# Fused causal attention and two-way max MoE on one core: score tiles of a head pair packed into three full PSUM tiles, three score regions per two pairs

## The chip, the cores and the metric

One core of a Trainium2 chip. The metric is the time of one execution on the device, in microseconds (us). Ratios are the mean time of one kernel's fast runs over the mean of the kernel before's fast runs of the same rounds, on the same chip, so they are not quite the ratio of the medians quoted beside them. A run is called slow where it lies over 1.5% above the fastest of its kernel. "Before" and "after" are the kernel without and with the change.

## The reference

Block-causal attention (blocks of 64, 8 batches, 8 heads, 576 positions, head size 64), then a feed-forward layer that takes the maximum of two projections.

```python
scores = scale * np.matmul(q, k.transpose(0, 1, 3, 2))
mask = block_i >= block_j                       # blocks of 64
scores = np.where(mask, scores, -1e9)
attn = np.exp(scores - scores.max(-1)) ; attn /= attn.sum(-1)
x = (attn @ v).transpose(0, 2, 1, 3).reshape(B * S, H * D)      # 4608 x 512
out = np.maximum(x @ w1, x @ w2) @ w_out
```
(Shortened; the kernel works in bf16 with float32 sums.)

## The kernel before

Two heads make a **pair**, 32 pairs in all; two pairs make a **group**. TensorE holds both heads of a pair side by side, one in each half of its 128 rows (64-row form). In the main loop (pairs 4 to 31) every pair goes to the scores twice (each such stretch in the 64-row form is a **visit**), and in between TensorE is filled with feed-forward matmuls of earlier batches (`fill(n)`) and with the attention-value product (`av`) of the pair two steps back. Scores live in two tiles of two banks in PSUM, the memory that TensorE writes its sums to; everything else shares four one-bank PSUM buffers (`ps_m`).

```python
    ps_s = ctx.enter_context(tc.tile_pool(name="ps_s", bufs=2, space=bass.MemoryType.PSUM))
    ps_m = ctx.enter_context(tc.tile_pool(name="ps_m", bufs=4, space=bass.MemoryType.PSUM))
# ... transposes(): two ps_m tiles, 18 small transposes; copy_out() empties the first on
#     VectorE and the second on ScalarE (`copies`)
    def burst_a(p):
        u0 = ps_s.tile([P, 2, 512], FP32, name="ps_s", tag="s")
        scores(p, u0, 0, 0, 0, 512)          # key chunk 0, 512 queries
        u1 = ps_s.tile([P, 2, 512], FP32, name="ps_s", tag="s")
        scores(p, u1, 0, 0, 512, 64)
        scores(p, u1, 64, 1, 128, 448)
        exp(p, u0, 512, 0)
        mask(p, 0)
        exp(p, u1, 512, 512)
        mask(p, 576)

    def burst_b(p):
        u2 = ps_s.tile([P, 2, 512], FP32, name="ps_s", tag="s")
        scores(p, u2, 0, 2, 256, 320)
        scores(p, u2, 320, 3, 384, 192)
        u3 = ps_s.tile([P, 2, 512], FP32, name="ps_s", tag="s")
        scores(p, u3, 0, 4, 512, 64)         # the last 64 keys: a tile of its own
        exp(p, u2, 512, 1024)
        # ... masks
        exp(p, u3, 64, 1536, m=BLK)
# ... main loop, per pair s:
        burst_a(s)
        fill(n_a)
        copy_out = t_pair(s)                 # transposes of the next group's queries or keys
        burst_b(s)
        copy_out()
        pool_work(s)
        if s >= HP + LAG:
            p = s - LAG
            av(p, [0, 1])
            fill(n_b)
            av(p, [2, 3, 4])
        fill(n - n_a - n_b)
```

The softmax here doesn't subtract the row's maximum and nothing guards it: scores larger than these inputs give would overflow.

## Time and profile before

| | before |
|---|---|
| median | 289.32 us (288.81 to 289.93, 3 runs) |
| span of the profiled run | 286.7 us |
| TensorE, VectorE, ScalarE, GpSimd busy | 98%, 65%, 48%, 35% |
| one group of the steady part | 15.56 us |

In profile lines PE is TensorE (PEld its weight loads), DVE is VectorE, ACT is ScalarE, POOL is GpSimd; L420 is a line of the kernel; `[...]` is idle time before an instruction and what the profile thinks ended it.

### The profile page before, as it was taken

Reading aid. Unit: us, or ns where it says so; the run is one execution under the profiler, and the core shown is the slowest. Engines: PE = TensorE matmul, PEld = TensorE weight load, DVE = VectorE, ACT = ScalarE, POOL = GpSimd, SP = SyncE. Lnnn points to the kernel's source line nnn. Section 1 sums busy time; section 2 is a strip of 40 time slices with the busy share of each in tenths; the row PEclk is TensorE's granted clock in tenths of the full one; section 3 lists DMA queues with packets and bytes.
Section 4 is the critical chain, followed back from the end, with each engine's and each line's share of the span. In section 5 each row is a group of like instructions: output and inputs, shape, how many; then the busy total and the mean of one; then the engine's idle time right before and its main releaser. Section 6 shows DMA issues by size and latency. Waiting matters only on the chain.

```text
span 286.7 us, 7670 instructions
## 1 busy us (share of the span) xinstructions
PE 280.0 (98%) x3197; PEld 146.1 (51%) x3197; DVE 186.7 (65%) x390; ACT 137.0 (48%) x194; POOL 101.5 (35%) x243
## 2 busy tenths in 40 slices
PE   7799999999999999999999999999999999999995
PEld 3457666555554545545445445454554554444443
DVE  6867878578785666766665666566665766455430
ACT  3786575775665455555545555545545100010112
POOL 2995547547535432344225532543111000000000
PEclk9999999999999999999999999999999999999999
DMA  7999999977954692479266684555101011011114
GB/s 266 259 210 233 169 259 257 247 231 86 192 133 82 141 144 88 156 77 237 49 201 75 171 115 105 130 59 67 43 37 39 37 39 74 37 63 49 53 60 146
DMA packets 55939, 36.67 MB, mean 128 GB/s; under 512 B 38752, under 2 KB 43232, under 8 KB 55904
## 3 DMA queue, kind: packets, MB, share of 16 engines
q0 software_dynamic: 41728, 7.87, 34.0%
q1 hardware_dynamic: 13760, 27.66, 28.4%
q10 hardware_dynamic: 416, 0.66, 0.7%
q8 instruction: 25, 0.41, 0.6%
q14 instruction: 10, 0.08, 0.1%
HBM read 34.60 MB, written 9.44 MB: 154 GB/s over the span
## 4 chain that ended last, share of the span: by engine, by line
PE 93%; DMA 4%; DVE 1%; POOL 0%; issue 0%; ACT 0%
PE ps_h L196 44%; PE ps_y L214 21%; PE ps_o L398 12%; PE ps_s L319 8%; DMA vv<-in_v_dram 2%; PE ps_qT L302 2%; DMA qraw<-in_q_dram 2%; PE ps_xe L420 2%; PE ps_kT L302 2%; PE ps_w L291 1%; PE ps_y L230 1%; PE ps_xo L422 0%; DVE g L205 0%; DVE xp L405 0%; POOL vv L131 0%; DVE qT L309 0%
## 5 line engine op out<-in xcount | busy, mean ns | idle before, releaser
L196 PE MATMUL ps_h<-xT,w_sb 128*128 128x512 bf16 (+3 forms) x640 | 140.7, 358 | 0.1
L325 ACT ACTIVATE aT<-ps_s 128x1024 bf16<-128x1024 f32 (+3 forms) x128 | 100.3, 832 | 59.5 <-PE ps_s L319 56.9
L196 PEld LDWEIGHTS <-w_sb 128*128 128x128 bf16 x640 | 57.7, 98 | 55.6 <-issue 5.5
L203 DVE CAST h<-ps_h 128x512 bf16<-128x512 f32 (+3 forms) x80 | 50.9, 636 | 44.6 <-PE ps_h L196 42.9
L214 PE MATMUL ps_y<-wo_sb,g 128*128 128x512 bf16 x280 | 69.6, 379 | 0.0
L330 POOL MEMSET aT<- 64x128 bf16 x124 | 22.7, 200 | 107.7 <-ACT aT L325 107.3
L220 ACT COPY y<-ps_y 128x512 f32<-128x512 f32 x31 | 18.2, 586 | 81.3 <-PE ps_y L214 58.8
L205 DVE TENSOR_TENSOR g<-h,ps_h 128x512 bf16<-128x512 bf16 (+3 forms) x80 | 50.5, 631 | 9.1 <-PE ps_h L196 7.4
L398 PEld LDWEIGHTS <-aT 128*128 128x128 bf16 x960 | 33.8, 98 | 14.8 <-DVE xp L405 7.6
L398 PE MATMUL ps_o<-vv,aT 128*128 128x65 bf16 x960 | 40.5, 194 | 0.3
L214 PEld LDWEIGHTS <-g 128*128 128x128 bf16 x280 | 25.5, 98 | 27.6 <-issue 3.2
L319 PE MATMUL ps_s<-qT,kT 64*128 64x64 bf16 (+6 forms) x400 | 34.7, 271 | 0.9 <-ACT kT L309 0.7
L131 POOL DMA_DIRECT2D vv<-in_v_dram x40 | 33.7, 847 | 0.0
L405 DVE TENSOR_TENSOR xp<-ps_o,rec 128x256 bf16<-128x256 f32 (+1 forms) x64 | 31.4, 491 | 2.2
L319 PEld LDWEIGHTS <-kT 64*128 64x128 bf16 x400 | 15.9, 94 | 15.2 <-issue 9.3
L404 DVE RECIPROCAL rec<-ps_o 128x4 f32<-128x4 f32 (+1 forms) x64 | 11.8, 184 | 15.1 <-PE ps_o L398 14.8
L127 POOL CAST qn<-qraw 128x1152 bf16<-128x1152 f32 (+1 forms) x15 | 16.5, 1102 | 7.2 <-DMA qraw<-in_q_dram 4.5
L127 POOL CAST kn<-kraw 128x1152 bf16<-128x1152 f32 x15 | 17.2, 1146 | 3.7 <-DMA kraw<-in_k_dram 2.9
L186 POOL COPY g<-g 128x512 bf16<-128x512 bf16 x8 | 4.9, 614 | 37.9 <-DVE g L205 37.8
L425 DVE COPY xT<-ps_xe 128x640 bf16<-128x640 bf16 (+2 forms) x18 | 8.1, 452 | 11.6 <-PE ps_xe L420 11.1
L309 DVE COPY qT<-ps_qT 128x576 bf16<-128x576 bf16 x17 | 12.9, 757 | 2.0 <-PE ps_qT L302 0.7
L309 DVE COPY kT<-ps_kT 128x576 bf16<-128x576 bf16 x17 | 12.8, 754 | 1.8 <-PE ps_kT L302 0.8
(41 smaller groups left out, 113.9 us busy)
## 6 DMA issues: line engine op xcount, KB each, us to landing
qraw<-in_q_dram SPq DMA_DIRECT2D x16, 576.0 KB, 4.2
out_dram<-y SPq DMA_DIRECT2D x35, 256.0 KB, 2.1
kraw<-in_k_dram SPq DMA_DIRECT2D x15, 576.0 KB, 6.1
vv<-in_v_dram POOLq DMA_DIRECT2D x32, 128.0 KB, 6.7
w_sb<-in_moe_w_dram POOLq DMA_DIRECT2D x4, 256.0 KB, 6.5
w_sb<-in_moe_w_dram POOLq DMA_DIRECT2D x2, 512.0 KB, 10.8
wo_sb<-in_moe_w_out_dram POOLq DMA_DIRECT2D x2, 512.0 KB, 12.0
kraw<-in_k_dram ACTq DMA_DIRECT2D x1, 576.0 KB, 5.4
```

The source lines that it names most:

```text
L127: copy(out=n[:, j0:j1], in_=t[:, j0:j1])
L131: nc.gpsimd.dma_start(out=vv_r[b % NV][:rows, c, :, :D], in_=v[b, :, c * P:c * P + rows, :].rearrange("h p d -> p h d"),)
L196: nc.tensor.matmul(pt[:, :w], w_sb[:, c, f * P:(f + 1) * P], xT[:, c, t0:t0 + w], start=(c == 0), stop=(c == NDM - 1),)
L203: nc.vector.tensor_copy(out=h1[:, :w], in_=pt[:, :w])
L205: nc.vector.tensor_max(g[:, f, m:m + w], h1[:, :w], pt[:, :w])
L214: nc.tensor.matmul(py[:], g[:, f, s * P:(s + 1) * P], wo_sb[:, f, :], start=(f == 0), stop=(f == NFF - 1),)
L309: copies[i](out=t[:, :S].rearrange("q (p j) -> q p j", j=RPP), in_=pts[i].rearrange("q j p -> q p j"),)
L319: nc.tensor.matmul(ps[:m, hh, col:col + w], kT[r, c * P:c * P + m], qT[r, q0:q0 + w], start=True, stop=True,)
L325: nc.scalar.activation(out=aT_r[p % NA][:m, :, a0:a0 + w], in_=ps[:m, :, :w], func=AF.Exp, scale=scale,)
L330: (eng or nc.gpsimd).memset(aT_r[p % NA][BLK:, :, a0:a0 + BLK], 0.0)
L398: nc.tensor.matmul(po[:, gi, hh, :], a[:, hh, a0:a0 + P], vv[:, c, h0 + 2 * hh, :], start=(mm == 0), stop=(mm == n_mm - 1),)
L405: nc.vector.tensor_mul(xp[:, ts[0]:ts[0] + n, :, p % 2], po[:, :, :, :D], rec[:, :n].to_broadcast([P, n, 2, D]),)
```

## The change

The last 64 keys see only the last 64 queries, a 64x64 piece per head that took a whole PSUM tile. Chunk 3 has a corner that the causal mask throws away anyway: its last 64 keys against queries 384 to 447. The change puts the piece there. Two matmuls with zero-padded keys (`kz` = keys 384 to 447, zeros, keys 512 to 575) accumulate the useful upper half and the piece in the lower half. Now a pair fills exactly three tiles, two pairs six, and two tiles make a **region**: three score regions per group instead of four. The attention-value work moves ahead of the transposes and the region.

```diff
+    def pad_keys(p):
+        nc.gpsimd.tensor_copy(  # blocks 0 and 2 of kz <- blocks 6 and 8 of the keys
+    def corner_scores(p, ps, col):
+        qT, kz = qT_r[p % NT], kz_r[p % NT]
+        for k0, q0 in ((0, 384), (BLK, 512)):
+            for hh in range(2):
+                r = slice(hh * D, (hh + 1) * D)
+                nc.tensor.matmul(
+                    ps[:, hh, col:col + BLK], kz[r, k0:k0 + P], qT[r, q0:q0 + BLK],
+                    start=(k0 == 0), stop=(k0 > 0),
+                )
+    def tile_2(p):
+        corner_scores(p, u, 320)
+        scores(p, u, 0, 2, 256, 320)
+        scores(p, u, 384, 3, 448, P)
+        # exp of all 512 columns, and of the corner's lower half to its own place
-    for s in range(HP, NPAIR):
-        burst_a(s) ; fill(n_a) ; t_pair(s) ; burst_b(s) ; av(...) ; fill(...)
+    for g in range(GPB, NG):
+        region(tile_0(a), tile_1(a))
+        lo, hi = n // 18, n * 2 // 9
+        for p, tiles in ((a, lambda: (tile_2(a), tile_0(b))), (b, lambda: (tile_1(b), tile_2(b)))):
+            fill(hi)
+            av_with(p - LAG, lo)             # av [0, 1], fill(lo), av [2, 3, 4]
+            copy_out = t_pair(p)
+            region(*tiles())                 # scores of both tiles, then both exps
+            copy_out()
+            # ... pad_keys for the next group, pool_work
+        fill(n - 2 * (lo + hi))
```
(Cut and joined; also moved: the rows of the last v chunk, some initial memsets, and the casts of queries and keys, now together once per group.)

More of the change, by code (lines that the diff above doesn't have):

```diff
@@ L94 @@
     qT_r = [ring.tile([P, S], BF16, name=f"qT{r}") for r in range(NT)]
-    kT_r = [ring.tile([P, S + APAD], BF16, name=f"kT{r}") for r in range(NT)]
+    kz_r = [ring.tile([P, 3 * BLK], BF16, name=f"kz{r}") for r in range(NT)]
+    kT_r = [ring.tile([P, S], BF16, name=f"kT{r}") for r in range(NT)]
     vv_r = [ring.tile([P, NCH, H, D + 1], BF16, name=f"vv{r}") for r in range(NV)]
@@ L131, in load_v @@
         nc.gpsimd.dma_start(
-            out=vv_r[b % NV][:rows, c, :, :D],
+            out=vv_r[b % NV][P - rows:, c, :, :D],
             in_=v[b, :, c * P:c * P + rows, :].rearrange("h p d -> p h d"),
@@ L161 @@
         nc.vector.memset(vv_r[r][:, :, :, D:D + 1], 1.0)
-        nc.vector.memset(vv_r[r][BLK:, NCH - 1, :, :], 0.0)
+        nc.vector.memset(vv_r[r][:BLK, NCH - 1, :, :], 0.0)
+    for r in range(NA):
+        nc.vector.memset(aT_r[r][:, :, AW:], 0.0)
     for r in range(NT):
-        nc.vector.memset(kT_r[r][:, S:], 0.0)
-    for r in range(NA):
-        nc.vector.memset(aT_r[r][BLK:, :, CB[4] + 512:], 0.0)
-        nc.vector.memset(aT_r[r][:BLK, :, AW:], 0.0)
+        nc.vector.memset(kz_r[r][:, BLK:2 * BLK], 0.0)
     cast("q", 0, ((dve, 0, 7), (pool, 7, RPP)))
@@ L313, in transposes, with scores @@
         return copy_out
-    def scores(p, ps, col, c, q0, w, m=P):
+    def scores(p, ps, col, c, q0, w):
         qT, kT = qT_r[p % NT], kT_r[p % NT]
+        k0 = min(c * P, S - P)
         for hh in range(2):
@@ L319, in scores, with exp @@
             nc.tensor.matmul(
-                ps[:m, hh, col:col + w], kT[r, c * P:c * P + m], qT[r, q0:q0 + w],
+                ps[:, hh, col:col + w], kT[r, k0:k0 + P], qT[r, q0:q0 + w],
                 start=True, stop=True,
             )
-    def exp(p, ps, w, a0, m=P):
+    def pad_keys(p):
+        nc.gpsimd.tensor_copy(
+            out=kz_r[p % NT].rearrange("p (a c) -> p a c", c=BLK)[:, 0:3:2],
+            in_=kT_r[p % NT][:, S - 3 * BLK:].rearrange("p (a c) -> p a c", c=BLK)[:, 0:3:2],
+        )
[7 more added lines that the diff above has]
+                    start=(k0 == 0), stop=(k0 > 0),
+                )
+    def exp(p, ps, w, a0):
         nc.scalar.activation(
-            out=aT_r[p % NA][:m, :, a0:a0 + w], in_=ps[:m, :, :w], func=AF.Exp, scale=scale,
+            out=aT_r[p % NA][:, :, a0:a0 + w], in_=ps[:, :, :w], func=AF.Exp, scale=scale,
         )
@@ L358, in masks_q, with tile_0, tile_1, out @@
             mask(p, a, eng)
-    def burst_a(p):
-        u0 = ps_s.tile([P, 2, 512], FP32, name="ps_s", tag="s")
-        scores(p, u0, 0, 0, 0, 512)
-        u1 = ps_s.tile([P, 2, 512], FP32, name="ps_s", tag="s")
-        scores(p, u1, 0, 0, 512, 64)
-        scores(p, u1, 64, 1, 128, 448)
-        exp(p, u0, 512, 0)
-        mask(p, 0)
-        exp(p, u1, 512, 512)
-        mask(p, 576)
-    def burst_b(p):
-        u2 = ps_s.tile([P, 2, 512], FP32, name="ps_s", tag="s")
-        scores(p, u2, 0, 2, 256, 320)
-        scores(p, u2, 320, 3, 384, 192)
-        u3 = ps_s.tile([P, 2, 512], FP32, name="ps_s", tag="s")
-        scores(p, u3, 0, 4, 512, 64)
-        exp(p, u2, 512, 1024)
-        mask(p, 1024)
-        mask(p, 1344)
-        exp(p, u3, 64, 1536, m=BLK)
+    def tile_0(p):
+        u = ps_s.tile([P, 2, 512], FP32, name="ps_s", tag="s")
+        scores(p, u, 0, 0, 0, 512)
+        return lambda: (exp(p, u, 512, 0), mask(p, 0))
+    def tile_1(p):
+        u = ps_s.tile([P, 2, 512], FP32, name="ps_s", tag="s")
+        scores(p, u, 0, 0, 512, 64)
+        scores(p, u, 64, 1, 128, 448)
+        return lambda: (exp(p, u, 512, 512), mask(p, 576))
+    def tile_2(p):
+        u = ps_s.tile([P, 2, 512], FP32, name="ps_s", tag="s")
+        corner_scores(p, u, 320)
+        scores(p, u, 0, 2, 256, 320)
+        scores(p, u, 384, 3, 448, P)
+        def out():
+            exp(p, u, 512, 1024)
+            nc.scalar.activation(
+                out=aT_r[p % NA][BLK:, :, 1536:AW], in_=u[BLK:, :, 320:320 + BLK],
+                func=AF.Exp, scale=scale,
+            )
+            mask(p, 1024)
+            mask(p, 1344)
+        return out
+    def region(*tiles):
+        for out in tiles:
+            out()
     def av(p, ts):
@@ L433, with fill_of @@
     KEEP = 6
-    def fill_of(s):
-        if s >= NPAIR - LAG:
-            return 27
-        left = 10 - s if s < 10 else 4 - (s - 2) % 4
+    def fill_of(g):
+        if g == NG - 1:
+            return 54
+        left = 5 - g if g < 5 else 2 - (g - 5) % 2
         return -(-max(0, ready() - KEEP) // left)
@@ L448, in pool_work @@
             cast("q", 4, ((pool, 0, RPP),))
+            cast("k", 4, ((pool, 0, RPP),))
         else:
@@ L451, in pool_work @@
                 load_qk(g + 3, (SP, SP), gated=True)
-            if g + 1 + i < NG:
-                cast("kq"[i], g + 1 + i, ((pool, 0, RPP),))
+            if i == 1 and g + 2 < NG:
+                cast("q", g + 2, ((pool, 0, RPP),))
+                cast("k", g + 2, ((pool, 0, RPP),))
             nb, j = divmod(s + 2, HP)
@@ L531 @@
     transposes("k", 2, (dve, act))()
+    pad_keys(4)
+    pad_keys(5)
     fill(2)
@@ L546, with av_with @@
     x_due = []
-    for s in range(HP, NPAIR):
-        g, i = divmod(s, 2)
+    def av_with(p, n):
+        av(p, [0, 1])
+        fill(n)
+        av(p, [2, 3, 4])
+    for g in range(GPB, NG):
+        a, b = 2 * g, 2 * g + 1
         if x_due:
             x_out(x_due.pop())
-        n = fill_of(s)
-        burst_a(s)
-        if s == HP:
+        n = fill_of(g)
+        region(tile_0(a), tile_1(a))
+        if g == GPB:
             av(3, [2, 3, 4])
@@ L556 @@
             x_out(1, 2, NCH)
-            n = fill_of(s)
-        n_a = n // 2 if n > 12 else n * 3 // 5
-        n_b = n // 6
-        fill(n_a)
-        copy_out = t_pair(s)
-        burst_b(s)
-        copy_out()
-        pool_work(s)
-        if s >= HP + LAG:
-            p = s - LAG
-            av(p, [0, 1])
-            fill(n_b)
-            av(p, [2, 3, 4])
-            if p % 2:
-                x_due.append(p // 2)
-        else:
-            fill(n_b)
-        fill(n - n_a - n_b)
+            n = fill_of(g)
+        lo, hi = n // 18, n * 2 // 9
+        for p, tiles in ((a, lambda: (tile_2(a), tile_0(b))), (b, lambda: (tile_1(b), tile_2(b)))):
+            fill(hi)
+            if g > GPB:
+                av_with(p - LAG, lo)
+            else:
+                fill(lo)
+            copy_out = t_pair(p)
+            region(*tiles())
+            copy_out()
+            if p % 2 and g + 1 < NG:
+                pad_keys(p + 1)
+                pad_keys(p + 2)
+            pool_work(p)
+        if g > GPB:
+            x_due.append(g - 1)
+        fill(n - 2 * (lo + hi))
     for p in range(NPAIR - LAG, NPAIR):
@@ L577 @@
             x_out(x_due.pop())
-        av(p, [0, 1])
-        fill(5)
-        av(p, [2, 3, 4])
+        av_with(p, 5)
         fill(11)
```

## The prediction

> **What bounds the kernel now.** I read the page first: the row of busy times, the slices, and the chain that ended last.
>
> ```profile
> PE 280.0 (98%) x3197; PEld 146.1 (51%) x3197; DVE 186.7 (65%) x390; ACT 137.0 (48%) x194; POOL 101.5 (35%) x243
> PE   7799999999999999999999999999999999999995
> PE 93%; DMA 4%; DVE 1%; POOL 0%; issue 0%; ACT 0%
> PE ps_h L196 44%; PE ps_y L214 21%; PE ps_o L398 12%; PE ps_s L319 8%; DMA vv<-in_v_dram 2%; PE ps_qT L302 2%; DMA qraw<-in_q_dram 2%; PE ps_xe L420 2%; PE ps_kT L302 2%; PE ps_w L291 1%; PE ps_y L230 1%; PE ps_xo L422 0%; DVE g L205 0%; DVE xp L405 0%; POOL vv L131 0%; DVE qT L309 0%
> ```
>
> TensorE is busy in every slice but the first and last ones and is 93% of the chain. So only what TensorE itself does, or what makes it pause between matmuls, can move the time; ACT at 48% and POOL at 35% matter only if they hold a buffer that TensorE wants. Busy time hides short pauses, because a matmul's modelled end lies some 0.2 to 0.4 us after its start. The view that shows pauses is the timeline of TensorE, read from start to start (columns: start us, us from first start to last end, then the operation and its count). This is one pair in the steady part:
>
> ```profile
> 152.74 0.59 PE L196 MATMUL ps_h<-xT,w_sb 128*128 128x512 bf16 x2
> 153.26 0.61 PE L319 MATMUL ps_s<-qT,kT 64*128 64x512 bf16 x6
> 153.80 2.76 PE L196 MATMUL ps_h<-xT,w_sb 128*128 128x512 bf16 x12
> 156.50 0.44 PE L302 MATMUL ps_kT<-ident,kn 64*128 64x64 bf16 x18
> 156.77 0.41 PE L319 MATMUL ps_s<-qT,kT 64*128 64x320 bf16 x6
> 157.12 0.36 PE L398 MATMUL ps_o<-vv,aT 128*128 128x65 bf16 x6
> 157.31 0.59 PE L196 MATMUL ps_h<-xT,w_sb 128*128 128x512 bf16 x2
> 157.78 0.59 PE L214 MATMUL ps_y<-wo_sb,g 128*128 128x512 bf16 x2
> 158.33 0.91 PE L398 MATMUL ps_o<-vv,aT 128*128 128x65 bf16 x24
> 159.08 1.46 PE L214 MATMUL ps_y<-wo_sb,g 128*128 128x512 bf16 x6
> 160.37 0.59 PE L196 MATMUL ps_h<-xT,w_sb 128*128 128x512 bf16 x2
> ```
>
> Six undisturbed 512-column matmuls take 160.37 - 159.08 = 1.29 us, 0.215 us each: my unit. What a stretch takes beyond such units is a pause. Two matmuls before the scores take 153.26 - 152.74 = 0.52 against 0.43: 0.09 us lost on entering the 64-row form (the label 64*128). The first score visit moves 512 + 64 + 448 = 1024 columns of each head, the two heads side by side in the two halves of the rows, so 0.43 us of streaming, and takes 0.54: 0.11 lost on leaving. The second visit repeats it: the twelve matmuls before it take 2.70 against 2.58 (0.12), and in it 18 transposes (0.27) and 576 columns of scores (0.24) take 157.12 - 156.50 = 0.62 (0.11). **So a visit to the 64-row form costs about 0.20 us besides its columns**, whatever is inside; transposes and scores in one visit share it.
>
> **What the Trainium skill says.** "TensorEngine Tiling (Array Packing)", Key Properties: "Changing tiling mode (not just tile) drains the TensorE". It gives no duration; the trace agrees, at about 0.1 us per change as just read. "TensorE: Matmul & The Clock Gate", Back-to-back issue gap, has N/2.4 + 2.5 ns warm, 216 ns at 512 columns; the trace has 215. "PSUM — Partial Sum Buffer", the four PSUM rules: a group's first matmul clears the written-bits of its whole bank. The new corner is an accumulation of two matmuls in a bank that other scores also use; it is issued first and finished before they start, so it stays right, and costs no wait. That no run has shown yet. "ScalarE: Activation LUTs", What ACT_TABLE_LOAD costs: an ACTIVATE takes 186 ns + 0.833 N, so 1039 ns at 1024 elements; the trace's exp of that size has 1022.
>
> **The change part by part.**
> 1. Score visits. Before, each pair of the main loop makes two visits, four per two pairs, and the transposes of the next queries or keys and the transposes of the finished output sit inside visits that exist anyway. After, two pairs make three visits; the transposes again stand directly before a score region. Pairs 4 to 31 are 28, 14 groups of two: 56 visits become 42. 14 x 0.20 us = **2.8 us less on TensorE, all of it on the chain**.
> 2. Score columns. Before: 512 + 64 + 448 + 320 + 192 + 64 = 1600 per head. After: 512 + 64 + 448 + 320 + 128 and two corner matmuls of 64 = 1600. Nothing gained. There are two more matmuls per pair, 56 in all, side by side in twos. The transposes of 64 columns run at 0.27 / 9 = 0.030 us per two, against 0.027 for the columns alone, so 28 x 0.003: **0.1 us more**; I allow 0.2 for the extra weight loads.
> 3. Exp. Three of 1024 elements and one of 128 per pair, before and after (1022 and 258 ns): the small one now reads a strip of the third tile in place of a fourth tile. ACT time is the same. What changes is that a region's ACT work becomes 2.04, 2.30, 2.30 us, where it was 2.04 and 1.28 per pair.
> 4. Zero-padded keys. One small POOL copy of 128 x 128 per pair; from POOL's 512-element copy (614 ns) and its 64x128 memset (200 ns) I estimate 0.25 us, 28 x 0.25 = 7 us on an engine with 185 us idle. Its reader comes a region later. **Zero on the path.** The regrouped casts and the moved rows of v are the same work.
> 5. Order of the attention-value matmuls. They used to follow the second visit; now they stand between plain matmuls and the transposes. The entering and leaving are in part 1, but their waits change. Before, 157.78 to 158.33 is 0.55 for two matmuls, 0.12 over, and 157.31 to 157.78 is 0.04 over: TensorE wants a PSUM buffer that VectorE still reads, after the key copy and the first output's normalization. The waits view names it:
>
> ```profile
> PEld L398 <- DVE xp L405: 7.6, 17, 0.5
> ```
>
> Those 7.6 us are the weight loader's idle time, mostly covered by matmuls; in matmul starts I read about 0.15 us per pair, some 3 to 4 us in all. After, VectorE has no copy to make just ahead of the first normalization, so part of that should go, about half, 1.5 us; but the transposes now want two buffers at once right after the second group, and I give back 0.8 us. Net **0.7 us less**.
>
> Sum: 289.3 - 2.8 + 0.2 - 0.7 = **286.0 us**; as buffers more often cost than give, I put it at **286.2 us**, 1.1% less.
>
> **The rivals.**
> *A. ScalarE's longer burst holds buffers.* The second transposed half is copied out by ACT behind the region's exps. Before, in the ACT timeline, the copy came 1.08 us after the first exp began:
>
> ```profile
> 157.28 1.18 ACT L325 ACTIVATE aT<-ps_s 128x1024 bf16<-128x1024 f32 x2 [1.59 <-PE ps_s L319]
> 158.36 0.62 ACT L309 COPY kT<-ps_kT 128x576 bf16<-128x576 bf16 x1
> ```
>
> After, it stands behind 2.3 us of exps, so one of the four general PSUM buffers is held a good 1 us longer, in 26 of 28 pairs, and a finished y tile can wait as long. Speaking for it: the buffer pauses of part 5 exist already, and VectorE is at 82% from 60 to 90 us. Against: between regions stand 10 + 2 unit matmuls (2.6 us) and 0.94 us of attention-value work in the steady part, and three buffers still rotate. If every such hold cost 0.15 us, it is 4 us: the gain is eaten, time about 289 to 290.
> *B. The regions come too close for two score buffers.* A region needs both, and so the exps of the region before: 0.5 us until the first starts, plus 2.3. Between region starts in the steady part lie some 0.5 + 2.6 + 0.94 + 0.27 = 4.3 us, and in the early stretch, with 16 unit matmuls per pair where the steady part has 24, still about 3.5. Slack 0.7 us at the worst, so no wait; if it were wrong for the three or four early groups, 0.5 us a region, 2 to 4 us, time 288 to 290.
> *C. The waits of part 5 vanish entirely.* With the attention-value work in a quiet stretch, all 3 to 4 us go: about 283.5 to 284.5.
>
> **Range and chances.** The visit term is counted from a constant that repeats in every pair, so I trust it to 0.3 us. The spread is the buffer waits, from C to A: 284.3 to 288.6 should hold 8 in 10. More than 2% faster needs 283.5 or less, that is C entirely and more: 6%. More than 2% slower needs 295.1, for which nothing in the profile speaks: 2%. Within 2%: 92%.
>
> **What the profile after would show.** Right: 42 score visits in the loop, three per two pairs in the timeline, each still 0.09 to 0.12 us over on entry and exit; 56 more score matmuls; TensorE still busy in all middle slices; the POOL copy of keys with nobody waiting. Parts 1 and 2 are wrong if entry or exit grows with the longer region, or the corner's matmuls take more than 0.03 us per two. Part 5 is right if two matmuls ahead of the attention-value work take 0.43 to 0.45. Rival A shows as pauses before the transposes, or before the matmuls after a region, with a copy by ACT ending just then; rival B as a pause before the scores that an exp ends. The prediction fails if these pauses sum to over 2.5 us, or if the early groups run longer than before.

## More of the kernel before

At the start of each group the finished attention output is transposed (tile `ps_xe`). The first such line of two successive groups in the timeline of TensorE (start, duration, operation, count) gives the period, 160.90 - 145.34 = 15.56 us, and it repeats to 0.01 us:

```profile
145.34 0.20 PE L420 MATMUL ps_xe<-ident,xp 64*128 64x64 bf16 x1
...
160.90 0.20 PE L420 MATMUL ps_xe<-ident,xp 64*128 64x64 bf16 x1
```

Every kernel here does 48 feed-forward matmuls in such a group, so periods compare directly. There are eight of them from about 83 us on, then one last group with 54 such matmuls and no transposes of queries and keys (15.99 us). Before them stand five groups with fewer; the last two, from 59.4 us on, have 32 feed-forward matmuls each in every kernel and took 11.90 and 11.83 us: the "early groups" below.

## The result, and the profile after

**286.5 us** (median of 4 runs: 286.56, 286.25, 286.45 and one slow run of 290.9 at a clock of 0.994) against 289.62 us before in the same rounds. Ratio of fast runs 0.9894, 95% interval 0.9865 to 0.9923: 1.1% faster, within 2%. Predicted: 286.2 us.

The page of the kernel after, its busy row, the slices of TensorE and the chain by engine:

```profile
PE 271.8 (95%) x3207; PEld 152.1 (53%) x3253; DVE 186.5 (65%) x386; ACT 140.8 (49%) x194; POOL 108.8 (38%) x271
...
PE   8799999899999999999999999999999999999995
...
PE 81%; issue 2%; ACT 2%; DVE 1%; ACTq 0%
```

TensorE seems to have become less busy. It has not: 3253 weight loads stand beside 3207 matmuls, where the kernel before had 3197 of each, so 46 matmul records are missing, many of them directly after a score region. The extra 56 weight loads are the 56 extra matmuls.

The timeline of TensorE after, one region of the steady part with what stands ahead of it, and two group starts:

```profile
144.96 0.20 PE L451 MATMUL ps_xe<-ident,xp 64*128 64x64 bf16 x1
...
152.45 0.35 PE L429 MATMUL ps_o<-vv,aT 128*128 128x65 bf16 x6
152.64 0.59 PE L197 MATMUL ps_h<-xT,w_sb 128*128 128x512 bf16 x2
153.20 0.89 PE L429 MATMUL ps_o<-vv,aT 128*128 128x65 bf16 x24
154.03 0.44 PE L303 MATMUL ps_kT<-ident,kn 64*128 64x64 bf16 x18
154.30 0.38 PE L321 MATMUL ps_s<-qT,kT 64*128 64x64 bf16 x4
154.52 0.22 PE L339 MATMUL ps_s<-qT,kz 64*128 64x64 bf16 x4
154.58 0.36 PE L321 MATMUL ps_s<-qT,kT 64*128 64x320 bf16 x4
...
160.15 0.20 PE L451 MATMUL ps_xe<-ident,xp 64*128 64x64 bf16 x1
```

The period is 15.19 us: 0.36 us less per group (15.20 in most). Of that, one visit saved explains about 0.20. The corner (four matmuls) takes 154.58 - 154.52 = 0.06 us. But the two feed-forward matmuls before `ps_o` take 153.20 - 152.64 = 0.56 us where they need 0.43. The timeline of all engines names what ended just then:

```profile
152.52 0.63 ACT L310 COPY qT<-ps_qT 128x576 bf16<-128x576 bf16 x1
...
153.20 0.89 PE L429 MATMUL ps_o<-vv,aT 128*128 128x65 bf16 x24
```

ScalarE's copy of the transposed half, begun at 152.52 behind the region's exps, ends at 153.15, and 0.05 us later TensorE goes on. This is the prediction's rival A, once per group. In the early groups the same place shows a longer pause:

```profile
66.26 0.69 DVE L206 TENSOR_TENSOR g<-h,ps_h 128x512 bf16<-128x512 bf16 x1 [0.17 <-PE ps_h L197]
...
66.46 0.38 PE L197 MATMUL ps_h<-xT,w_sb 128*128 128x512 bf16 x1
...
67.00 0.47 PE L429 MATMUL ps_o<-vv,aT 128*128 128x65 bf16 x10 [0.16 <-DVE g L206]
```

One matmul from 66.46 to 67.00 is 0.54 us where it needs 0.215: 0.32 us lost. Here TensorE waits for the buffer that VectorE's maximum reads; ScalarE's copy holds another of the four until 67.62. The group before these two (from 49.66 us) lost most, at the key transposes, and there the label names the copy. Timeline of TensorE:

```profile
55.95 0.20 PE L303 MATMUL ps_kT<-ident,kn 64*128 64x64 bf16 x1
56.55 0.42 PE L303 MATMUL ps_kT<-ident,kn 64*128 64x64 bf16 x17 [0.40 <-ACT qT L310]
```

The scores follow at 56.80, so the 18 transposes took 0.85 us where they take 0.27 elsewhere (154.03 to 154.30): 0.58 us lost. So the steady groups gained 0.36 us each, and the early ones lost a little: 11.93 and 11.94 us against 11.90 and 11.83, and 10.63 against 10.11 in the group before them.

**Theory.** The gain is the saved visit (0.20 us x 14) plus buffer waits of the old order that went away; the new order brought waits of its own, and I took them all to come from ScalarE's copy, which stands behind more exps. **Rival 1:** the order and its waits explain everything, visits cost nothing. **Rival 2:** visits explain everything and the waits are hidden or only move.

### The profile page after: what moved, and what is told of

Read it like the earlier page. It is cut to its first block, busy times and chain, and to the rows that moved or that the text cites. A ratio compares the mean times of both kernels' runs of the same rounds, so it can differ in the third digit from the quotient of the medians.

```text
span 284.7 us, 7763 instructions
## 1 busy us (share of the span) xinstructions
PE 271.8 (95%) x3207; PEld 152.1 (53%) x3253; DVE 186.5 (65%) x386; ACT 140.8 (49%) x194; POOL 108.8 (38%) x271
## 4 chain that ended last, share of the span: by engine, by line
PE 81%; issue 2%; ACT 2%; DVE 1%; ACTq 0%
PE ps_h L197 39%; PE ps_y L215 21%; PE ps_o L429 9%; PE ps_s L321 6%; PE ps_qT L303 2%; PE ps_kT L303 2%; PE ps_xe L451 2%; ACT aT L345 1%; DVE g L206 1%; PE ps_y L231 1%; PE ps_s L339 1%; ACT qT L310 0%; ACT aT L401 0%; ACT kT L310 0%; PE ps_xo L453 0%
## 5 line engine op out<-in xcount | busy, mean ns | idle before, releaser
L197 PE MATMUL ps_h<-xT,w_sb 128*128 128x512 bf16 (+3 forms) x604 | 133.8, 357 | 4.0 <-issue 3.2
L345 ACT ACTIVATE aT<-ps_s 128x1024 bf16<-128x1024 f32 (+2 forms) x100 | 95.9, 993 | 62.1 <-PE ps_s L321 50.2
L215 PE MATMUL ps_y<-wo_sb,g 128*128 128x512 bf16 x273 | 65.5, 379 | 0.8 <-issue 0.5
L429 PEld LDWEIGHTS <-aT 128*128 128x128 bf16 x960 | 37.0, 98 | 15.0 <-issue 3.9
L215 PEld LDWEIGHTS <-g 128*128 128x128 bf16 x280 | 27.0, 98 | 32.1 <-issue 1.1
L321 PE MATMUL ps_s<-qT,kT 64*128 64x64 bf16 (+6 forms) x344 | 31.8, 279 | 1.1 <-ACT kT L310 0.7
L321 PEld LDWEIGHTS <-kT 64*128 64x128 bf16 x344 | 13.6, 95 | 6.4 <-issue 2.8
```

Of the source, the lines that this page charges most:

```text
L197: nc.tensor.matmul(pt[:, :w], w_sb[:, c, f * P:(f + 1) * P], xT[:, c, t0:t0 + w], start=(c == 0), stop=(c == NDM - 1),)
L215: nc.tensor.matmul(py[:], g[:, f, s * P:(s + 1) * P], wo_sb[:, f, :], start=(f == 0), stop=(f == NFF - 1),)
L321: nc.tensor.matmul(ps[:, hh, col:col + w], kT[r, k0:k0 + P], qT[r, q0:q0 + w], start=True, stop=True,)
L345: nc.scalar.activation(out=aT_r[p % NA][:, :, a0:a0 + w], in_=ps[:, :, :w], func=AF.Exp, scale=scale,)
L429: nc.tensor.matmul(po[:, gi, hh, :], a[:, hh, a0:a0 + P], vv[:, c, h0 + 2 * hh, :], start=(mm == 0), stop=(mm == n_mm - 1),)
```

## The experiments

All were correct, and each was timed in five rounds beside the kernel before. They were timed in three batches, each on a chip of its own (a1 to b1; a4 to a7; b2 to a8), so between batches compare ratios and periods, not medians. Period is that of the steady groups.

| run | edit | median us | ratio (95% interval) | period us |
|---|---|---|---|---|
| after | | 286.50 | 0.9894 (0.9865-0.9923) | 15.20 |
| a1_again | after, once more | 286.94 | 0.991 (0.9886-0.9935) | 15.20 |
| a2_split_one | one region split | 288.76 | 0.9976 (0.9944-1.0008) | 15.28 |
| a3_split_three | three regions split | 293.36 | 1.014 (1.0097-1.0183) | 15.64 |
| b1_order | before, new order only | 288.14 | 0.9949 (0.9927-0.9971) | 15.27 |
| a4_lo_plus | after, one more matmul in the attention-value work | 284.57 | 0.9853 (0.9834-0.9872) | 15.01 |
| a5_lo_plus2 | two more | 288.07 | 0.997 (0.9957-0.9983) | 15.20 |
| a6_pad_thrice | padded keys copied three times | 287.14 | 0.9933 (0.9917-0.9949) | 15.20 |
| a7_copy_first | after, ScalarE copies ahead of the exps | **283.48** | **0.9812** (0.9799-0.9825) | 15.07 |
| b2_order_copy | before, new order and copy first | 287.79 | 0.994 (0.9909-0.9971) | 15.21 |
| b3_copy | before, copy first only | 285.94 | 0.9896 (0.9858-0.9935) | 15.22 |
| a9_split_three_copy | copy first, three regions split | 291.26 | 1.0071 (1.0031-1.011) | 15.64 |
| a8_corner_thrice | copy first, corner issued three times | 286.87 | 0.9928 (0.9882-0.9975) | 15.30 |

### Is a visit paid? a1_again, a2_split_one, a3_split_three

```diff
+    def apart():
+        fill(1)
+        return lambda: None
-        ... (tile_2(a), tile_0(b)) ...
+        ... (tile_2(a), apart(), tile_0(b)) ...     # a2; a3 the same in all three regions
```

(The last `fill` of the group is one or three shorter, so the number of matmuls stays.)

> The changed kernel once more, as the measure for the others on the same chip. Both theories: 286.5 us (286.2 to 286.8), ratio to before 0.990.

> The changed kernel with one plain matmul moved between the two tiles of each group's second region, so that every two pairs make four score visits again; columns, exps, corner and order of the attention-value work stay. Theory that visits are paid by their number, 0.20 us each: 14 x 0.20 = +2.8 us, 289.3 us. Rival, that the gain is in the moved attention-value work and its waits alone: no change, 286.5 us.

> The same in all three regions: six visits per two pairs. Theory of a fixed price per visit: 42 x 0.20 = +8.4 us, 294.9 us, three times the step of the split in one region. Rival, waits alone: 286.5 us.

The repetition gave 286.94 us, as expected within its spread. Splitting one region cost 1.8 us by the medians, splitting three 6.4 us. Rival 1 is refuted: the order of the attention-value work was untouched. But both steps are smaller than 2.8 and 8.4. The periods say why: a2 adds only 0.08 us per group, because shifting one matmul also removed the 0.135 us wait (0.20 - 0.135 = 0.07); from a2 to a3, 0.36 us for two visits. The last group, in which no transposes and so no ScalarE copies happen, shows the price undisturbed: 15.99 us before, 15.78 after (205.75 to 221.53), 15.99 with one split, 16.42 with three. That is **0.21 us per visit**, three times over. In the timelines of TensorE before and after:

```profile
207.57 0.20 PE L420 MATMUL ps_xe<-ident,xp 64*128 64x64 bf16 x1
223.56 0.20 PE L420 MATMUL ps_xe<-ident,xp 64*128 64x64 bf16 x1
...
205.75 0.20 PE L451 MATMUL ps_xe<-ident,xp 64*128 64x64 bf16 x1
221.53 0.20 PE L451 MATMUL ps_xe<-ident,xp 64*128 64x64 bf16 x1
```

The profiled run of a3 had a clock of 0.94 from 30 to 60 us (0.994 on the mean) but counts as fast by the 1.5% rule; without it the ratio of a3 is 1.012. Its groups from 90 us on ran at 1.00.

### Is the order worth something by itself? b1_order

```diff
         fill(n_a)
+        av(p, [0, 1]) ; fill(n_b) ; av(p, [2, 3, 4])
         copy_out = t_pair(s)
         burst_b(s)
         copy_out()
         pool_work(s)
-        av(p, [0, 1]) ; fill(n_b) ; av(p, [2, 3, 4])
```

> The kernel before with only the attention-value work moved ahead of the transposes and the second score visit, as in the changed kernel; four visits and four score tiles stay. The traces show 0.32 us per two pairs of waits ahead of that work before, in 10 groups of the steady part. If they go and few come back: 286.0 to 287.3 us. If the number of visits explains the whole gain: 289.4 us. By my prediction's part 5 (0.7 us): 288.7 us.

288.14 us: more than the prediction's 0.7 us, less than I expected now. The steady period fell by 0.29 us, nearly the whole 0.32 us of waits. But the early groups grew, from 11.90 and 11.83 to 12.34 and 12.25 us (and the first steady one was 15.70). There the output transposes, two of the small PSUM tiles at once, come right behind the region. In the timeline of all engines:

```profile
71.97 0.62 ACT L309 COPY kT<-ps_kT 128x576 bf16<-128x576 bf16 x1
...
72.64 0.19 PE L422 MATMUL ps_xo<-ident,xp 64*128 64x64 bf16 x1 [0.32 <-ACT kT L309]
```

The copy ends at 72.59, the output transposes go on at 72.64, with the copy as label. Again a buffer held by ScalarE's copy.

### Filling the wait: a4_lo_plus, a5_lo_plus2

```diff
-        lo, hi = n // 18, n * 2 // 9
+        lo, hi = n // 18 + 1, n * 2 // 9        # a4;  + 2 in a5
```

> The changed kernel with one more plain matmul between the two parts of each attention-value work (three in place of two in the steady groups, two in place of one in the early ones). Theory: its second part waits for a PSUM buffer until a fixed moment, 0.135 us in each of 10 steady groups (the buffer that ScalarE's copy of the transposed half holds) and 0.32 us in each of 3 early groups (VectorE's maximum); a matmul of 0.215 us fills that time. -1.35 - 3 x 0.21 = -2.0 us: 284.9 us where the changed kernel has 286.9. Rival, that the gain of the change is the number of visits only and these waits are hidden or move elsewhere: 286.9 us.

> The same with two more. Theory: the steady wait is already gone, the early one goes wholly: a further -0.3 us, 284.6 us. Rival, waits move: 286.9 us or more.

a4 came out as expected in all: 284.57 us, period 15.20 to 15.01; but in the early groups (12.15 and 11.58 us against 11.93 and 11.94) the gain was 0.14 us over both, where 0.21 in each was expected. a5 did not: 288.07 us. My theory of a wait until a fixed moment failed there. As I read the program, one more matmul ends a feed-forward unit inside the attention-value work, the next unit takes a buffer, and the second part of that work is left with the one that ScalarE holds. Timeline of all engines, early group:

```profile
68.53 0.63 ACT L310 COPY qT<-ps_qT 128x576 bf16<-128x576 bf16 x1
...
69.21 0.89 PE L429 MATMUL ps_o<-vv,aT 128*128 128x65 bf16 x24 [0.41 <-ACT qT L310]
```

The wait is now 0.57 us and plainly labelled. So shifting matmuls is luck; what has to go is the long hold.

### Is GpSimd on the path? a6_pad_thrice

```diff
-                pad_keys(p + 1)
-                pad_keys(p + 2)
+                for _ in range(3):
+                    pad_keys(p + 1)
+                    pad_keys(p + 2)
```

> The changed kernel with each copy of the padded keys on GpSimd made three times: 56 more copies of 0.29 us, 16 us more of GpSimd. Theory that this engine is off the path: 286.9 us, no change. Rival, that GpSimd's queue delays masks or casts that TensorE comes to wait for: at least 0.3 us per group, 291 us.

The row of the copy in the kernel after (count, busy us, mean ns; idle time before it):

```profile
L328 POOL COPY kz<-kT 128x128 bf16<-128x128 bf16 x28 | 8.1, 293 | 4.3 <-ACT kT L310 3.4
```

16 us more of these gave the same period, 15.20 us, in steady groups, 11.93 and 11.94 us in early ones, and 287.14 us, whose interval overlaps that of a1_again. No cost of the padded keys is seen.

### Taking the hold away: a7_copy_first

```diff
             copy_out = t_pair(p)
-            region(*tiles())
-            copy_out()
+            outs = tiles()                    # scores of both tiles
+            copy_out()
+            region(*outs)                     # then the exps
```

> The changed kernel with the copies of the transposed halves issued ahead of the region's exps on ScalarE, so that the buffer comes free some 2.3 us earlier, at the price of exps that start 0.63 us later. Theory (rival A of the prediction, seen as the 0.135 us wait in steady groups): that wait goes, -1.3 us, 285.6 us, perhaps less if the early groups gain as well. If ScalarE's hold is not what the work waits for: 286.9 us. If the later exps are missed: slower, 287.5 us or more.

**283.48 us**, 1.9% faster than before: better than both kernels and than I expected. Timelines of TensorE and of ScalarE, the same place of a group:

```profile
149.91 0.35 PE L429 MATMUL ps_o<-vv,aT 128*128 128x65 bf16 x6
150.09 0.59 PE L197 MATMUL ps_h<-xT,w_sb 128*128 128x512 bf16 x2
150.52 0.90 PE L429 MATMUL ps_o<-vv,aT 128*128 128x65 bf16 x24
151.35 0.44 PE L303 MATMUL ps_kT<-ident,kn 64*128 64x64 bf16 x18
```

```profile
151.93 0.64 ACT L310 COPY kT<-ps_kT 128x576 bf16<-128x576 bf16 x1 [1.10 <-PE ps_kT L303]
152.47 1.95 ACT L345 ACTIVATE aT<-ps_s 128x1024 bf16<-128x1024 f32 x2
```

The two matmuls take 0.43 us, no wait. The copy starts 0.58 us after its transposes began (151.35 to 151.93) where it stood behind 2.3 us of exps. The steady period fell by 0.13 us, as the wait foretold; the early groups by 0.28 us, to 11.66, since their wait for VectorE's buffer also went (65.00 to 65.22 us in its timeline, one matmul, no pause); that another buffer was free in its place is my reading, the trace does not name buffers. Against a1_again the ratio fell by 0.0098, 2.8 us (2.4 against the first timing's 0.9894): what the late copy cost the changed kernel. The group starts say the same: from 29.80 to 84.16 us the changed kernel took 54.36 us, a7 52.74 (29.41 to 82.15), and 1.06 us more over the eight steady groups, 2.7 us in all.

### The same cure on the kernel before: b3_copy, and packing alone: b2_order_copy

```diff
-    def burst_b(p):
+    def burst_b(p, copy_out):
         scores(p, u3, 0, 4, 512, 64)
+        copy_out()
         exp(p, u2, 512, 1024)
```

> The kernel before with one thing changed: ScalarE's copy of the transposed half is issued ahead of the second visit's exps. Theory that the waits ahead of the attention-value work (0.12 + 0.04 us per pair) exist because that copy keeps a buffer: the larger of them goes in 20 steady pairs, -2.4 us, 286.6 us. Rival, that only VectorE's key copy and normalization cause them: 289.0 us.

> The kernel before with the attention-value work moved ahead of the transposes and with ScalarE's copy ahead of the second visit's exps: the same order and the same absence of buffer waits as the run with the copy first (283.5 us), but four visits and four score tiles. So the difference of the two is the packing alone. Theory of a price per visit: 14 x 0.20 - 0.1 = 2.7 us, 286.2 us. Rival, that without waits the visits cost nothing more: 283.5 us.

b3: 285.94 us, period 15.22, a little more than expected: both waits of the kernel before go, 0.34 us per group. Timeline of TensorE in b3, the lines that answer to the place shown of before:

```profile
164.77 0.35 PE L399 MATMUL ps_o<-vv,aT 128*128 128x65 bf16 x6
164.96 0.60 PE L196 MATMUL ps_h<-xT,w_sb 128*128 128x512 bf16 x2
165.40 0.59 PE L214 MATMUL ps_y<-wo_sb,g 128*128 128x512 bf16 x2
165.83 0.88 PE L399 MATMUL ps_o<-vv,aT 128*128 128x65 bf16 x24
```

0.44 and 0.43 us where it was 0.47 and 0.55. The label `DVE xp` of the waits view, which I had followed, named what TensorE took in the end; what made it wait there was ScalarE's late copy. By itself this one-line reordering is worth as much as the whole change, within the intervals (0.9896 against 0.9894). (The profiled run of b3, 287.51 us, is one of its two slower runs. Its steady groups repeat to 0.01 us; its loop's first output transposes began at 31.75 us, where a7's did at 29.41.)

b2 differs from a7 by the packing and by what moved with it: four feed-forward matmuls, not two, between the two parts of the attention-value work, and the casts, memsets and v rows. No run moves those by themselves. In the steady groups there is little room for an effect of theirs: 15.56 - 0.32 (old waits) - 0.20 (a visit) + 0.01 (corner) + 0.13 (new wait) = 15.18, measured 15.20. The steady period of b2 is 0.20 us above the best packed one (15.21 against 15.01 in a4) and 0.15 above a7's. Of the 0.06 between a7 and a4, 0.04 lies in the query transposes, 0.31 us in a7 (146.85 to 147.16) and 0.27 in a4 and b2; what holds them is not shown. The time was 287.79 where I expected 286.2. In the early groups a wait appeared that I had not counted (12.22 and 11.92 us):

```profile
77.99 1.18 ACT L325 ACTIVATE aT<-ps_s 128x1024 bf16<-128x1024 f32 x2
...
79.07 0.39 PE L319 MATMUL ps_s<-qT,kT 64*128 64x512 bf16 x2
```

The next visit wants a score tile that the large exp, begun at 77.99 and 1.02 us long, still reads: 79.01, and the scores start at 79.07. With four visits per group and the exps 0.6 us later, visits here come too close for two score tiles; three visits leave room. That is the prediction's rival B, in a kernel that it was not written for, and a second use of the packing. The profile gives this wait no label; the start times show it. So in the order of b1 the copy first gained nothing that shows (0.994 against 0.9949): the cure depends on what the delayed exps hold in turn. It is 0.16 us in each of the two early groups, so only a part of the 1.6 us that I missed; the periods put most of the rest before the steady part too, and I have not broken it down.

### Once more without waits: a9_split_three_copy; and the corner: a8_corner_thrice

a9 splits a7 as a3 split after; a8 issues `corner_scores` three times in a7.

> The kernel with the copy first, its three regions each split by one plain matmul: six visits per two pairs, now without the buffer waits that blurred the earlier split. Theory of 0.20 us per visit: 42 x 0.20 = +8.4 us, 291.9 us. If a visit costs only the 0.15 us that the earlier split gave: +6.4 us, 289.9 us.

> The kernel with the copy first, its corner scores issued three times (the same values written again): 28 x 4 more twos of 64-column matmuls. Theory of 0.030 us per two, as the transposes have: +3.4 us, 286.9 us. Rival, that accumulating onto the place just written drains, some 0.1 us per corner: +5.6 us more, 292 us or above.

a9: 291.26 us, period 15.64, 0.63 us over a4's for three visits, 0.21 each (0.57 over its parent a7's, 0.19 each, but a9's query transposes take 0.27 us as a4's do); by the ratios 7.5 us for 42, 0.18 each. The fixed price holds, near 0.20. a8: 286.87 us, as expected to 0.03 us (a match between two chips that proves little, and one of its runs had a clock of 0.994); 0.23 us per group for eight more twos, 0.029 us per two, so accumulating into the place just written cost nothing extra here.

## Why the prediction was right

**The number and the signs.** The number came true, but two signs by which the prediction itself would have failed came true as well. The late copy's pauses cost 2.7 us by the group starts (2.4 to 2.8 by the ratios), where it allowed 2.5, and the early groups ran longer than before (10.63, 11.93 and 11.94 us against 10.11, 11.90 and 11.83). The step that failed is the case against rival A, that the matmuls between the regions and three other buffers would cover the longer hold. That the total agreed all the same is luck, told under part 5.

**Bound.** Right: only TensorE's own work and its pauses moved the time. 16 us more on GpSimd did not.

**Part 1, visits.** Right, in mechanism and size: predicted 0.20 us each and 2.8 us in all; shown 0.21 in the group without copies, 0.20 and 0.21 in wait-free steady groups, 0.14 to 0.18 where splits are timed as a whole and waits shift with them.

**Part 2, columns and matmuls.** Right: 0.029 us per two of 64-column matmuls against the predicted 0.030. Every run with the corner gave correct results.

**Part 3, exp.** The amount was right. "A region's ACT work becomes 2.04, 2.30, 2.30 us" was noted there and its consequence put into rival A. Rival A was real: it cost the changed kernel 2.4 to 2.8 us, not the 0.8 us that part 5 gave back for new waits, though less than the 4 us that the rival itself named. The gain survived it because the old order's waits, of the same origin, went.

**Part 4, padded keys.** Right: 0.29 us per copy where 0.25 was estimated, nothing on the path.

**Part 5, order.** The net was about right by two errors that cancel. I took "about half, 1.5 us" of the old waits to go; over the eight steady groups all went (0.32 us in each, 2.6 us). I gave back 0.8 us; 2.7 us came back, as a7_copy_first shows: 0.13 us in each steady group, 1.1 us, and 1.6 us in the five groups before, more than the 1.0 us of their saved visits (5 x 0.20). Of the sign set for this part, 0.43 to 0.45 us for the two matmuls ahead, one pair of a group kept to it (148.14 to 148.57) and the other did not (0.56). The cause was wrong as well: I put the old waits down to VectorE's key copy and normalization. b3_copy shows that ScalarE's late copy was behind them. The sum with the sizes shown is -2.8 (visits) + 0.1 (matmuls) - 2.6 + 2.7 (waits) = -2.6 us, against a measured -2.6 us (a1_again's ratio) to -3.1 us (the medians).

**Rival B** did not show in the changed kernel: no score matmul carries an exp as its label. As b2 shows, such a wait can go unlabelled; but the sum above and the 0.32 us found in an early group leave next to no room for it there. (Its cost was also summed too low: 0.5 us in each of three regions of three or four groups is 4.5 to 6 us, not 2 to 4.) **Rival C** did not happen either, but a7_copy_first shows what it would have been: 283.5 us, the lower end of C's 283.5 to 284.5.

## What to carry to other kernels

Count how often TensorE changes between the 64-row and the 128-row form, read the price of one change from start-to-start times in the timeline, and merge visits; a packing that saves a PSUM tile is worth it mainly because it lets visits merge. When a PSUM buffer is emptied by an engine that also has long work queued, issue the short emptying copy first, and check what the delayed work holds in turn: here that was one line, worth as much as the whole repacking, and the two together gave 1.9%. A wait labelled with one engine can be caused by another that keeps the remaining buffers, so try the hold, not only the label.

## What the Trainium skill lacked or had wrong

- "TensorEngine Tiling (Array Packing)", Key Properties, says that changing the tiling mode drains the engine and gives no duration. Here entering cost about 0.10 us and leaving about 0.11 us, 0.21 us per visit in the group without other waits, for merged and split visits alike.
- "PSUM — Partial Sum Buffer", Engine vs sequencer instructions, has ScalarE's queue as strict FIFO, and its summary says to evacuate promptly; no page puts the two together as an order of issue or gives a size. Here a 0.63 us copy queued behind 2.3 us of exps held one of four buffers and cost 2.4 to 2.8 us of 286.9.
- "GPSIMD Engine Reference" names the copy among GpSimd's operations without a time for it: the 128x128 bf16 copy took 0.293 us.
- "ScalarE: Activation LUTs" gives 1039 ns for an exp of 1024 elements by its formula; the traces have 1022 to 1023 ns, close enough.
